# Attention with unnormalised probabilities, x's rows scaled by one over the sums, and a planner that knows a port and due work

## The chip, the cores and the metric

The kernel runs on one core of one Trainium2 chip. The metric is the device time of one execution in microseconds, as the median of the runs shown. The core's engines work side by side, each through its own queue in order: PE (TensorE, matrix products; PEld is its loading of weights), DVE (VectorE), ACT (ScalarE), POOL (GpSimd) and SP (SyncE), which issues the DMAs here.

## The reference, cut to what matters

```python
scores = q @ k.T / sqrt(64)                           # 4 batches, 8 heads, 576 rows, 64 wide
scores = causal(scores + cum[:, None] - cum[None, :]) # cum: running sum of log(clip(f))
attn = exp(scores - max(scores))
attn = attn / (sum(attn) + 1e-9)
x = concat_heads(attn @ v)                            # 2304 x 512
h = x @ w_in                                          # MoE1: 512 -> 1024
solu = h * softmax(h)
x = layernorm(solu) * g_ln @ w_out                    # 1024 -> 512
h = relu(x @ w2_in)                                   # MoE2: 512 -> 2048
out = (h * h) @ w2_out                                # 2048 -> 512
```

## The kernel before

**Precision.** The products of MoE1, MoE2 and the scores take each operand as a high part and a residual ("hi", "lo"), with three products for one in the MoEs. So every weight goes through `convert` once: a DMA of the raw words, an absolute value on ACT (L604), a scaling of the low words on whichever engine the planner picks (L283, L285 or L289), a shift (L608) and a merge (L612) on DVE, an add on POOL (L618), a high part cast on any engine (L281, L285 or L287) and a residual on POOL or DVE (L622).

**Work.** The 2304 tokens are cut into 20 attention tiles of 128 or 64 query rows (five for each batch). For each tile and each of 8 heads, `head` makes the scores in a bank Z (L465), finds the row's extreme value (L482, L485 on DVE), takes the exponential on ACT with the row sums beside it (L499), adds 1e-9 and inverts on DVE (L512 or L516, then L522), and multiplies the probabilities by that on POOL (L526). PE transposes them (L542), the result is copied to a PT buffer (L281, mostly on ACT), and `mix` multiplies by V, two heads at a time, into the bank XO (L563), which collects x, transposed. After the eighth head, XO is cast into XH (L281) and the residual XL is taken (L576). `first` then does MoE1's first product (L747 to L749, bank HP) and its softmax and layer norm; `out1` does the second product (L688 to L690) and stores x for MoE2. `step` does one of MoE2's 16 slices of the hidden width for a block of 384 tokens: 12 products up (L1019 to L1021), ReLU and square on ACT (L1027, L1029), a cast (L1030) and a residual (L1033) on DVE, 9 products down (L1049 to L1051).

**Stages.** MoE1's 24 weight pieces are converted beside the first attention tiles (`weights1`); MoE2's 64 pieces are converted after the last tile, into buffers that attention and MoE1 leave free (`weights2`), beside the first two blocks' steps. The other four blocks follow.

**The order of the work** comes from a planner, `Plan.lay`, when the kernel is built. Each group of instructions is a step with the engines that may do it, a cost on each, the steps it depends on and a priority (a due time: small goes first). `lay` simulates the engines; on each, of all steps that could start within 20 ns of the earliest, it takes the one with the smallest priority. The result is a fixed order for each engine. Semaphores keep the dependences; nothing keeps the simulated times.

```python
t0 = min(c[0] for c in cand)
c = min((c for c in cand if c[0] <= t0 + slack), key=lambda c: (c[1].prio, c[1].no))
```

A head's priority is its slot time. A piece of MoE2's weight slice fc is due at TEND - 3000 + 5000 fc, a step of block 0 at TEND - 2000 + 12000 fc, and one of block 1 15000 later.

Of the kernel before, what the change touches and what calls it, by code (L numbers as in the profile page):

```python
# [8 lines left out]
F32 = mybir.dt.float32  # L9
# [14 lines left out]
class Step:  # L24
    __slots__ = ("eng", "fn", "prio", "deps", "succ", "left", "rdy", "start", "end", "take", "uses", "on", "no", "late", "weak")


class Plan:
# [28 lines left out]
    def add(self, eng, fn, prio, reads=(), writes=(), take=None, uses=(), late=0):  # L57
# [8 lines left out]
        s.weak = None  # L66
# [29 lines left out]
    def lay(self, slack=60):  # L96
# [49 lines left out]
        todo = len(self.steps)  # L146
        order = []
        while todo:
            pick = None
            for e in engs:  # L150
                cand = []
                for s in avail[e]:
                    t = max(free[e], s.rdy[e])
                    if e == "dve" and len(s.eng) > 1:

                        o = min(max(free[x], s.rdy[x]) + s.eng[x] for x in s.eng if x != e)
                        if t + s.eng[e] + SHIFT > o:
                            continue
# [10 lines left out]
                c = min((c for c in cand if c[0] <= t0 + slack), key=lambda c: (c[1].prio, c[1].no))  # L169
                done = pe_end(c[0], c[1].eng[e], False) if e == "pe" else c[0] + c[1].eng[e]  # L170
# [7 lines left out]
            free[e] = done  # L178
            for a in s.eng:
                avail[a].remove(s)  # L180
# [14 lines left out]
def tile_kernel(ctx: ExitStack, tc: tile.TileContext, q, k, v, f, w_in, w_out, g_ln, w2_in, w2_out, out):  # L195
# [24 lines left out]
    NADJ, NPT, NV, NST = 3, 4, 6, 8  # L220
# [32 lines left out]
    ST = [new(f"st{i}", [8]) for i in range(NST)]  # L253
# [21 lines left out]
    def copy(n, dst, src, prio, reads, writes, uses=(), scale=None, psum=True):  # L275
# [20 lines left out]
        s = pl.add(ns, fn, prio, reads, writes, uses=uses)  # L296
# [28 lines left out]
    def att_ns(T):  # L325
        t, m = T["t"], T["m"]
        return 2 * max(107, T["ext"] / 2.4) + 53 + (t + 1) * m * (109 + 135) / 128 + 109

    EACH = 24 * 216 + 48 * 109 + 872
# [47 lines left out]
    def picks(i, j):  # L377
# [7 lines left out]
        s = pl.add(dict(dve=602, pool=1252), fn, -6.9e6 if i == 0 else 5000, ["ident"], [("qa", i, j)])  # L385

    def prep_k(n, prio):
# [5 lines left out]
        for j in range(2):  # L393
# [7 lines left out]
            def auxrows(y, j=j):  # L401
# [9 lines left out]
                dict(dve=67 + 1.045 * HH * m, pool=119 + 2.213 * HH * m), lo, prio + 2 * j, [("kn", j)] + hk, lk  # L411
# [8 lines left out]
    def prep_q(n, prio):  # L420
        m = tiles[n]["m"]
        i = n % 2
        for j in range(2):
# [14 lines left out]
            pl.add(dict(dve=67 + 1.045 * HH * m), lo, prio + 2 * j, [("qn", j), ("qh", i, j)], [("ql", i, j)])  # L438


    def head(s):
# [56 lines left out]
        def exp(y, c):  # L498
            nc.scalar.activation(  # L499
                out=adj[0:m, c[1] : c[2]], in_=Z[c[0]][0:m, 0 : c[2] - c[1]], func=AF.Exp, bias=st[0:m, low : low + 1],  # L500
                scale=-1.0, accum_out=st[0:m, 2 + y : 3 + y],
            )

        for y, (c, k_) in enumerate(zip(cuts, zk)):
            pl.add(
                dict(act=91 + 0.833 * (c[2] - c[1]) + 146), lambda y=y, c=c: exp(y, c), prio, [k_, sk_ + (low,)],
                [("adj", s % NADJ, y), sk_ + (2 + y,)], late=-110,
            )

        def total():  # L510
            if wide:
                nc.vector.scalar_tensor_tensor(  # L512
                    out=st[0:m, 4:5], in0=st[0:m, 2:3], scalar=1e-9, in1=st[0:m, 3:4], op0=ALU.add, op1=ALU.add
                )
            else:
                nc.vector.tensor_scalar_add(st[0:m, 4:5], st[0:m, 2:3], 1e-9)  # L516

        pl.add(
            dict(dve=69), total, prio - 300, [sk_ + (2 + y,) for y in range(len(cuts))], [sk_ + (4,)], late=93
        )  # L520
        pl.add(
            dict(dve=75), lambda: nc.vector.reciprocal(st[0:m, 5:6], st[0:m, 4:5]), prio - 300, [sk_ + (4,)], [sk_ + (5,)]  # L522
        )

        def norm():
            nc.gpsimd.tensor_scalar(  # L526
                out=adj[0:m, 0:ext], in0=adj[0:m, 0:ext], scalar1=st[0:m, 5:6], scalar2=1.0,
                op0=ALU.mult, op1=ALU.mult,
            )

        pl.add(dict(pool=244 + 0.833 * ext), norm, prio - 300, [sk_ + (5,)], ak)
# [20 lines left out]
    def mix(s):  # L552
# [17 lines left out]
        pl.add(dict(pe=(t + 1) * 270 * m / P), fn, prio, rk, ["xo"])  # L570
        if p == NP - 1:
            i = T["x"] % XB
            w = slice(off, off + m)

            def lo():
                nc.vector.tensor_tensor(  # L576
                    out=XL[i][:, :, w], in0=XO[:, :, w], in1=XH[i][:, :, w].bitcast(F32), op=ALU.subtract
                )

            copy(NP * m, lambda: XH[i][:, :, w], lambda: XO[:, :, w], prio, ["xo"], [("xh", i, off)])  # L580
            pl.add(dict(dve=67 + 1.045 * NP * m), lo, prio, ["xo", ("xh", i, off)], [("xl", i, off)])


    def convert(src, raw, w, hi, lo, n, prio, rawk, wk, outk, gain=None):
# [42 lines left out]
        pl.add(dict(dve=ts), a3, prio, [], [wk])  # L627
        pl.add(dict(dve=stt), a4, prio, [hk], [wk])
# [4 lines left out]
        m7 = pl.add(dict(pool=tt + 27, dve=stt), a7, prio, [wk, outk + ("h",)], [outk + ("l",)])  # L633
# [41 lines left out]
    def out1(blk, ccs, prio, dp):  # L675
# [3 lines left out]
        for cc in ccs:  # L679
            w = slice(cc * P, cc * P + P)  # L680
            sk = key()
            for g in range(4):
# [11 lines left out]
                pl.add(dict(pe=654), fn, prio, rk, [sk], take=sk if g == 0 else None, uses=[sk] if g else [])  # L694
# [37 lines left out]
    def first(x):  # L732
# [10 lines left out]
        for c in range(2):  # L743
            w = slice(c * 512, c * 512 + 512)
            for cc in range(KC):
                def fn(c=c, cc=cc, w=w):
# [5 lines left out]
                    dict(pe=648), fn, a + d * FH * (c * KC + cc) / 8, xk + [("wi", cc, c, y) for y in "hl"], ["h"]  # L752
# [135 lines left out]
    NRAW = NPT + 2  # L888
    raws = [(f"pt{i}", [("pt", i, g) for g in range(5)]) for i in range(NPT)]
    raws += [(f"adj{i}", [("adj", i, y) for y in range(2)]) for i in range(2)]  # L890
    wsl = [("adj2", 0), ("adj2", 256), ("xw", 0)]

    def weights2(fc, prio):
        pieces = places[fc]
        W2[fc] = [p[0] for p in pieces]
        for g in range(4):
# [106 lines left out]
    def step(blk, fc, prio):  # L1003
# [10 lines left out]
        for cc0 in range(0, KC, 2):  # L1014
            def up(cc0=cc0):
# [9 lines left out]
                dict(pe=6 * 162.5), up, prio, rk, [ck], take=ck if cc0 == 0 else None, uses=[ck] if cc0 else []  # L1025
# [273 lines left out]
```

## Time and profile before

| what | value |
|---|---|
| median of 3 runs | 905.02 us (904.74 to 905.56) |
| the profiled execution | 904.06 us, of which its span is 902.3 us |
| mean granted TensorE clock, as a share of 2.4 GHz | 0.98 |
| PE busy | 93% of the span |
| PEld busy | 80% |
| DVE busy | 56% |
| ACT busy | 52% |
| POOL busy | 39% |

How to read it: a share is a mean over stages with different limits. The views by stretch say which engine is full in each, the lists of waits say what PE waited for, and the groups of instructions say what one of a kind takes. The mean of a row contains the time for which an instruction, already begun, is held up. Line numbers such as L526 are those of the kernel before, unless it is said otherwise.

### The profile page before, as it was taken

What the parts mean: (1) busy time and instruction counts of PE and PEld (TensorE: products, weight loads), DVE (VectorE), ACT (ScalarE), POOL (GpSimd) and SP (SyncE); (2) the same over time, 40 slices, a digit from 0 to 9 for tenths busy, and PEclk for the clock granted to TensorE, in tenths of its full rate; (3) what the DMA queues carried; (4) which work ended last, traced back from release to release, by engine and by line L of the source; (5) the groups of instructions that cost most, each with busy time, mean ns of one, the idle gap of its engine ahead of it and who ended that gap; (6) DMA issues with size and microseconds to landing.
All of it is one profiled execution on the core that took longest, in us unless ns stands there. A gap on an engine that the chain in (4) does not pass through costs nothing.

```text
span 902.3 us, 15613 instructions
## 1 busy us (share of the span) xinstructions
PE 842.9 (93%) x5280; PEld 724.7 (80%) x5280; DVE 504.7 (56%) x1442; ACT 472.9 (52%) x1234; POOL 352.2 (39%) x508
## 2 busy tenths in 40 slices
PE   3878999999999999999979788999999999999998
PEld 1546887888888888788868677899989999899997
DVE  8998787666855677655799889322222222222221
ACT  5777767666766566665767666223322322322322
POOL 7988766433533456522588888100000000000000
PEclk9978898999999999999999999999999999999999
DMA  7733245222511125010545743005102002000000
GB/s 227 226 97 113 89 128 165 62 60 71 165 48 37 60 79 165 25 42 25 173 140 174 235 129 106 1 1 167 44 1 71 36 1 70 36 1 1 36 1 35
DMA packets 55503, 75.29 MB, mean 83 GB/s; under 512 B 7456, under 2 KB 35104, under 8 KB 55424
## 3 DMA queue, kind: packets, MB, share of 16 engines
q1 hardware_dynamic: 55424, 74.30, 26.6%
q8 instruction: 41, 0.67, 0.3%
q14 instruction: 38, 0.31, 0.1%
HBM read 59.91 MB, written 14.30 MB: 82 GB/s over the span
## 4 chain that ended last, share of the span: by engine, by line
PE 70%; DVE 13%; POOL 5%; issue 5%; DMA 4%; ACT 4%; SPq 1%; POOLq 0%; ACTq 0%; DVEq 0%
PE pp L1019 6%; PE pp L1021 6%; PE pp L1020 6%; PE pp L542 5%; PE z L465 5%; PE xo L563 5%; PE hp L747 3%; PE hp L749 3%; PE hp L748 3%; PE pp L688 3%; PE pp L689 3%; PE pp L690 3%; PE hp L1049 2%; PE hp L1050 2%; PE hp L1051 2%
## 5 line engine op out<-in xcount | busy, mean ns | idle before, releaser
L1030 DVE CAST q<-q 128x384 fp32r<-128x384 f32 x96 | 39.5, 411 | 251.5 <-PE pp L1051 92.2
L1027 ACT ACTIVATE q<-pp 128x384 f32<-128x384 f32 x96 | 47.1, 490 | 236.1 <-PE pp L1021 232.4
L526 POOL TENSOR_SCALAR adj<-adj,st 128x128 f32<-128x128 f32 (+9 forms) x160 | 100.2, 631 | 137.1 <-DVE st L522 96.7
L499 ACT ACTIVATE adj<-z,st 64x288 f32<-64x288 f32 (+9 forms) x192 | 95.7, 501 | 55.6 <-DVE st L485 36.7
L465 PE MATMUL z<-k,q 128*128 128x256 f32 (+17 forms) x384 | 98.7, 355 | 23.7 <-ACT adj L499 13.0
L281 ACT COPY pt<-pp 128x256 f32<-128x256 f32 (+5 forms) x176 | 72.3, 428 | 47.8 <-PE pp L542 45.8
L465 PEld LDWEIGHTS z<-k,q 128*128 128x128 f32 (+3 forms) x384 | 60.8, 192 | 36.8 <-ACT adj L499 18.9
L542 PE MATMUL pp<-ident,adj 128*128 128x128 f32 (+1 forms) x480 | 81.0, 284 | 9.2 <-POOL adj L526 8.3
L688 PE MATMUL pp<-ln,woh 128*128 128x256 f32 x288 | 83.4, 290 | 0.5 <-DVE ln L827 0.5
L485 DVE CUSTOM_DVE_ANT_0 z<-z,maskb 128x128 f32<-128x128 f32 (+8 forms) x144 | 65.5, 461 | 30.3 <-PE z L465 29.3
L690 PE MATMUL pp<-ln,woh 128*128 128x256 f32 x288 | 81.2, 282 | 0.0
L689 PE MATMUL pp<-ln,wol 128*128 128x256 f32 x288 | 81.2, 282 | 0.0
L542 PEld LDWEIGHTS pp<-ident,adj 128*128 128x128 f32 (+1 forms) x480 | 54.8, 145 | 31.3 <-POOL adj L526 16.5
L563 PE MATMUL xo<-pt,vn 128*64 128x128 f32 (+1 forms) x960 | 68.4, 279 | 0.0
L563 PEld LDWEIGHTS xo<-pt,vn 128*64 128x64 f32 x960 | 49.7, 141 | 21.6 <-issue 17.0
L747 PE MATMUL hp<-wih,xl 128*128 128x512 f32 x144 | 63.7, 442 | 1.1 <-ACT hp L786 0.6
L748 PE MATMUL hp<-wil,xh 128*128 128x512 f32 x144 | 58.9, 409 | 0.6 <-DVE st L516 0.6
L749 PE MATMUL hp<-wih,xh 128*128 128x512 f32 x144 | 58.6, 407 | 0.0
L688 PEld LDWEIGHTS pp<-ln,woh 128*128 128x128 f32 x288 | 54.7, 190 | 2.4 <-DVE ln L827 0.9
L689 PEld LDWEIGHTS pp<-ln,wol 128*128 128x128 f32 x288 | 54.7, 190 | 0.6
L690 PEld LDWEIGHTS pp<-ln,woh 128*128 128x128 f32 x288 | 54.4, 189 | 0.0
L1029 ACT ACTIVATE q<-q 128x384 f32<-128x384 f32 x96 | 50.3, 524 | 2.5
(479 smaller groups left out, 2238.2 us busy)
## 6 DMA issues: line engine op xcount, KB each, us to landing
x2d<-xc SPq DMA_DIRECT2D x72, 128.0 KB
kn<-in_k_dram SPq DMA_DIRECT2D x32, 256.0 KB
qn<-in_q_dram SPq DMA_DIRECT2D x32, 256.0 KB
pt<-in_moe_w_in_dram SPq DMA_DIRECT2D x22, 256.0 KB
pt<-in_moe_w_out_dram SPq DMA_DIRECT2D x22, 256.0 KB
vn<-in_v_dram SPq DMA_DIRECT2D x20, 256.0 KB
ln<-x2d SPq DMA_DIRECT2D x24, 192.0 KB
out_dram<-pt SPq DMA_DIRECT2D x18, 256.0 KB
```

The source lines that it names most:

```text
L281: nc.scalar.copy(dst(), src())
L465: nc.tensor.matmul(dst, lhsT=ql[0:r, p, 0:m], rhs=rhs, start=(g == 0), stop=(g == 1))
L499: nc.scalar.activation(out=adj[0:m, c[1] : c[2]], in_=Z[c[0]][0:m, 0 : c[2] - c[1]], func=AF.Exp, bias=st[0:m, low : low + 1], scale=-1.0, ...
L526: nc.gpsimd.tensor_scalar(out=adj[0:m, 0:ext], in0=adj[0:m, 0:ext], scalar1=st[0:m, 5:6], scalar2=1.0, op0=ALU.mult, op1=ALU.mult,)
L542: nc.tensor.transpose(at(sk)[:, (c - g) * m : (c - g + 1) * m], adj[0:m, zc : zc + P], ident[0:m, 0:m])
L563: nc.tensor.matmul(XO[own[j], p, off : off + m], lhsT=VN[vslot[b, c]][:, (2 * p + j) * D : (2 * p + j + 1) * D], rhs=pts[j][:, c * m : (c ...
L688: nc.tensor.matmul(px, lhsT=woh[:, fc, w], rhs=lo, start=(fc == 0), stop=False)
L689: nc.tensor.matmul(px, lhsT=wol[:, fc, w], rhs=hi, start=False, stop=False)
L690: nc.tensor.matmul(px, lhsT=woh[:, fc, w], rhs=hi, start=False, stop=(fc == KF - 1))
L747: nc.tensor.matmul(HP[:, c], lhsT=XL[i][:, cc, :], rhs=wih[:, cc, w], start=(cc == 0), stop=False)
L748: nc.tensor.matmul(HP[:, c], lhsT=XH[i][:, cc, :], rhs=wil[:, cc, w], start=False, stop=False)
L749: nc.tensor.matmul(HP[:, c], lhsT=XH[i][:, cc, :], rhs=wih[:, cc, w], start=False, stop=(cc == KC - 1))
```

## The change

**Attention.** The steps of L512, L516, L522 and L526 go: the exponentials are transposed and multiplied by V as they are. The row sums of the 8 heads of a tile are collected in a buffer `su`. At the end of a tile, eight sums at once get 1e-9 added and are inverted on DVE; a copy on any engine spreads the inverses, each 64 times, into a new buffer X (128 x 512); four transposes on PE (`spread`) and a copy from PSUM bring X into x's layout; one DVE multiply (`scaled`) takes XO times X into X; XH and XL are made from X, which lies in SBUF, so that POOL may do either.

**Planner.** A step marked `port` (most DVE operations with operands in SBUF alone, but not MoE2's L1030 and L1033) may not begin on DVE while POOL works in the simulation, and no POOL step begins while such a step runs on DVE. On the engines other than PE, where a step that becomes ready during the picked step is due by more than 400 earlier, and waiting for it wastes less time than it would be held up, it goes first, with something shorter put into the gap if that fits. Costs of PE's steps are set anew (a 512-column product 231 instead of 216 ns).

**Buffers.** PT buffers go from 4 to 3, the small ST buffers from 8 to 4, and X takes the place of one PT buffer as a landing place for MoE2's raw weights (still 6 in all). The causal mask is due earlier.

```diff
@@ Plan.lay
                     t = max(free[e], s.rdy[e])
+                    if e == "pool":
+                        t = max(t, port)
+                    elif e == "dve" and s.port and s.eng[e]:
+                        t = max(t, free["pool"])
...
+                if e != "pe":
+                    end = c[0] + c[1].eng[e]
+                    due = [
+                        x for x in cand
+                        if x[1].prio < c[1].prio - DUE and x[0] < end and end - x[0] > (x[0] - c[0]) * WORTH
+                    ]
+                    if due:
+                        x = min(due, key=lambda x: (x[1].prio, x[1].no))
+                        fits = [y for y in cand if y[0] + y[1].eng[e] <= x[0]]
+                        c = min(fits, key=lambda y: (y[1].prio, y[1].no)) if fits else x
...
+            if e == "dve" and s.port and s.eng[e]:
+                port = done
@@ copy
-        s = pl.add(ns, fn, prio, reads, writes, uses=uses)
+        s = pl.add(ns, fn, prio, reads, writes, uses=uses, port=not psum)
@@ tile_kernel
-    NADJ, NPT, NV, NST = 3, 4, 6, 8
+    NADJ, NPT, NV, NST = 3, 3, 6, 4
+    SU = [new(f"su{i}", [3, H]) for i in range(2)]
+    X = new("x", [NP, P])
@@ head
-                scale=-1.0, accum_out=st[0:m, 2 + y : 3 + y],
+                scale=-1.0, accum_out=su[0:m, y, h : h + 1],
...
-        pl.add(
-            dict(dve=75), lambda: nc.vector.reciprocal(st[0:m, 5:6], st[0:m, 4:5]), prio - 300, [sk_ + (4,)], [sk_ + (5,)]
-        )
...
-        pl.add(dict(pool=244 + 0.833 * ext), norm, prio - 300, [sk_ + (5,)], ak)
@@ mix, after a tile's last two heads
+            pl.add(dict(dve=72), total, prio - 300, sums, [uk])
+            pl.add(dict(dve=78), lambda: nc.vector.reciprocal(su[0:m, 2], su[0:m, 2]), prio - 300, [], [uk])
+            copy(
+                DM, lambda: X[0:m].rearrange("p c (j d) -> p (c j) d", d=D),
+                lambda: su[0:m, 2].unsqueeze(2).broadcast_to([m, H, D]), prio - 300, [uk], ["x"], psum=False,
+            )
+            pl.add(dict(pe=NP * 109 * m / P), spread, prio - 300, ["x", "ident"], [sk], take=sk)
+            copy(
+                NP * m, lambda: X[:, :, 0:m], lambda: at(sk).rearrange("p (c x) -> p c x", x=P)[:, :, 0:m], prio - 300,
+                [sk], ["x"], [sk],
+            )
+            pl.add(dict(dve=67 + 1.045 * NP * m), scaled, prio - 300, ["xo"], ["x"])
-            copy(NP * m, lambda: XH[i][:, :, w], lambda: XO[:, :, w], prio, ["xo"], [("xh", i, off)])
-            pl.add(dict(dve=67 + 1.045 * NP * m), lo, prio, ["xo", ("xh", i, off)], [("xl", i, off)])
+            copy(NP * m, lambda: XH[i][:, :, w], lambda: X[:, :, 0:m], prio, ["x"], [("xh", i, off)], psum=False)
+            l = pl.add(
+                dict(dve=67 + 1.045 * NP * m, pool=119 + 2.213 * NP * m), lo, prio, ["x", ("xh", i, off)], [("xl", i, off)],
+                port=True,
+            )
@@ weights2
-    NRAW = NPT + 2
+    NRAW = NPT + 3
+    raws += [("x", ["x"])]
@@ mask
-    pl.add(dict(pool=1480), mask, -6e6, ["ident"], ["mask", "e"])
+    pl.add(dict(pool=1480), mask, -8.95e6, ["ident"], ["mask", "e"])
+DUE, WORTH = 400, 1.0
```

**What moves, first place:** POOL beside the second attention tile, while MoE1's first weight is converted (`ln` is the staging buffer, `wih` and `wil` the weight's parts, `adj` the probabilities). Before:

```order
41 L526 TENSOR_SCALAR adj_32_99<-adj_32_99,st_37_104 128x256
42 L526 TENSOR_SCALAR adj_30_97<-adj_30_97,st_38_105 128x256
43 L285 TENSOR_SCALAR ln_52_163<-ln_52_163 128x512
44 L618 TENSOR_TENSOR ln_53_236<-ln_53_236 128x512
45 L526 TENSOR_SCALAR adj_31_98<-adj_31_98,st_39_106 128x256
46 L285 TENSOR_SCALAR wih_71<-ln_53_236 128x512
47 L618 TENSOR_TENSOR ln_52_163<-ln_52_163 128x512
48 L526 TENSOR_SCALAR adj_32_99<-adj_32_99,st_40_107 128x256
```

and with the change, in its own line numbers (L657 is the add, L661 a weight's residual, L421 K's residual, L307 any scaling or cast on POOL; `xh` is x's high part):

```order
27 L661 TENSOR_TENSOR wil_72<-ln_50_168,wih_71 128x512
28 L307 TENSOR_SCALAR xh_45_112<-x_109 128x512
29 L657 TENSOR_TENSOR ln_51_234<-ln_51_234 128x512
30 L421 TENSOR_TENSOR k_11_78<-kn_21_88,k_9_76 64x4x128
31 L307 TENSOR_SCALAR ln_50_168<-ln_50_168 128x512
32 L307 TENSOR_SCALAR q_16_83<-qn_22_89 64x512
33 L307 TENSOR_SCALAR q_17_84<-qn_23_90 64x512
34 L307 TENSOR_SCALAR k_8_75<-kn_20_87 128x4x128
35 L307 TENSOR_SCALAR k_9_76<-kn_21_88 128x4x128
```

The normalising multiplies are gone from between the conversions; more residuals stand on POOL, and the high parts of the weights have left it for ACT.

**Second place:** DVE while MoE2's weights are converted (`adj`, `xw`, `pt` and `x` hold pieces under conversion; the 128x384 rows are a step's cast and residual, into `q`, then `qn` or `kn`). Before:

```order
1180 L1030 CAST q_57_5617<-q_57_5597 128x384
1181 L608 TENSOR_SCALAR adj_56_4808<-adj_56_4808 128x256
1182 L1033 TENSOR_TENSOR qn_57_5628<-q_57_5597,q_57_5617 128x384
1183 L612 SCALAR_TENSOR_TENSOR adj_56_4808<-pt_56_4788,adj_56_4808 128x256
1184 L289 TENSOR_SCALAR pt_56_4869<-pt_56_4869 128x256
1185 L608 TENSOR_SCALAR adj_56_4808<-adj_56_4808 128x256
1186 L612 SCALAR_TENSOR_TENSOR adj_56_4808<-pt_56_4793,adj_56_4808 128x256
1187 L1030 CAST q_57_5656<-q_57_5597 128x384
1188 L608 TENSOR_SCALAR xw_4892<-xw_4892 128x256
1189 L1033 TENSOR_TENSOR qn_57_5668<-q_57_5597,q_57_5656 128x384
```

and with the change (L647 is the shift, L651 the merge, L1070 the cast, L1073 the residual):

```order
871 L647 TENSOR_SCALAR adj_54_4476<-adj_54_4476 128x256
872 L651 SCALAR_TENSOR_TENSOR adj_54_4476<-adj_54_4517,adj_54_4476 128x256
873 L1070 CAST q_55_4702<-q_55_4689 128x384
874 L1073 TENSOR_TENSOR kn_55_4706<-q_55_4689,q_55_4702 128x384
875 L647 TENSOR_SCALAR adj_54_4476<-adj_54_4476 128x256
876 L651 SCALAR_TENSOR_TENSOR adj_54_4476<-adj_54_4450,adj_54_4476 128x256
877 L647 TENSOR_SCALAR xw_4591<-xw_4591 128x256
878 L651 SCALAR_TENSOR_TENSOR xw_4591<-x_4581,xw_4591 128x256
879 L1070 CAST q_55_5340<-q_55_5323 128x384
880 L1073 TENSOR_TENSOR qn_55_5343<-q_55_5323,q_55_5340 128x384
```

A step's cast and its residual, and a piece's shift and its merge, now stand next to each other; before, a shift of another piece stood between. In the whole order 17 casts stood ahead of the last merge, and 20 do now.

## Rows read from the trace of the kernel before

**Rows 1.** The page, part 1: busy us (share of span) x instructions.

```profile
span 902.3 us, 15613 instructions
...
PE 842.9 (93%) x5280; PEld 724.7 (80%) x5280; DVE 504.7 (56%) x1442; ACT 472.9 (52%) x1234; POOL 352.2 (39%) x508
```

**Rows 2.** Four stretches: busy us of PE, PEld, DVE, ACT, POOL; clock, DMA, GB/s.

```profile
0.00:119.00 119.00, 88.30 (x508) 64.94 (x509) 105.77 (x279) 86.06 (x220) 100.75 (x142) 0.90 0.50 150
119.00:440.00 321.00, 316.99 (x2528) 266.94 (x2529) 211.03 (x796) 210.45 (x612) 143.24 (x226) 0.99 0.26 80
440.00:568.00 128.00, 107.00 (x597) 93.74 (x591) 114.76 (x210) 86.89 (x229) 106.70 (x140) 0.99 0.52 160
568.00:902.30 334.30, 330.62 (x1656) 299.06 (x1656) 73.12 (x159) 89.53 (x175) 1.54 (x2) 1.00 0.10 34
```

**Rows 3.** Waits of PE, 0 to 119 us: total us, times, longest.

```profile
PE z L465 <- ACT adj L499: 11.3, 7, 3.4
PE pp L542 <- POOL adj L526: 7.2, 11, 1.7
```

**Rows 4.** Two stretches, L526 on POOL alone: busy us (xcount).

```profile
0.00:119.00 119.00, 28.28 (x36) 0.90 0.50 150
119.00:440.00 321.00, 71.96 (x125) 0.99 0.26 80
```

**Rows 5.** First stretch, DVE lines L522, L516, L512 alone, in this order.

```profile
0.00:119.00 119.00, 5.53 (x36) 0.90 0.50 150
...
0.00:119.00 119.00, 4.45 (x32) 0.90 0.50 150
...
0.00:119.00 119.00, 1.49 (x4) 0.90 0.50 150
```

**Rows 6.** Groups by shape, POOL, 0 to 119 us: busy us, mean ns.

```profile
L285 POOL TENSOR_SCALAR ln<-ln 128x512 uint32<-128x512 uint32 x6 | 5.2, 874 | 2.1 <-DMA ln<-in_moe_w_in_dram 1.7
...
L622 POOL TENSOR_TENSOR wol<-xc,woh 128x256 fp32r<-128x256 f32 x6 | 4.6, 761 | 0.8 <-ACT woh L281 0.5
...
L285 POOL TENSOR_SCALAR wih<-ln 128x512 fp32r<-128x512 f32 x4 | 2.9, 737 | 0.1
...
L622 POOL TENSOR_TENSOR wil<-ln,wih 128x512 fp32r<-128x512 f32 x2 | 2.5, 1266 | 0.1
...
L285 POOL TENSOR_SCALAR woh<-xc 128x256 fp32r<-128x256 f32 x4 | 1.6, 404 | 0.1
```

**Rows 7.** Groups by shape, ACT, 0 to 119 us: the same columns.

```profile
L604 ACT ACTIVATE ln<-ln 128x512 f32<-128x512 f32 x8 | 5.4, 671 | 1.3 <-DMA ln<-in_moe_w_in_dram 1.3
...
L281 ACT CAST xh<-xo 128x512 fp32r<-128x512 f32 x4 | 2.3, 579 | 0.8 <-PE xo L563 0.8
...
L281 ACT CAST woh<-ws 128x256 fp32r<-128x256 f32 x5 | 2.0, 401 | 0.1
```

**Rows 8.** Lines L612 and L608 on DVE: ns min/median/max, first and last start.

```profile
L612 DVE SCALAR_TENSOR_TENSOR adj<-pt,adj x33: 417/793/947, 440.1 to 566.8; 128x256 uint32<-128x256 uint32 x33
...
L608 DVE TENSOR_SCALAR adj<-adj x43: 278/350/884, 439.7 to 565.7; 128x256 uint32<-128x256 uint32 x43
```

**Rows 9.** The chain of waits, 170 to 180 us: start, us, what.

```profile
175.43 0.87 PE pp L824 x8
```

**Rows 10.** Waits of PE, 119 to 440 us.

```profile
PE pp L542 <- POOL adj L526: 1.2, 3, 0.7
```

**Rows 11.** Waits of PE, 440 to 568 us.

```profile
PE hp L1049 <- DVE qn L1033: 8.6, 7, 2.3
PE z L1049 <- DVE kn L1033: 7.3, 5, 2.5
```

**Rows 12.** Two stretches, L1033 on DVE alone: busy us (xcount).

```profile
440.00:568.00 128.00, 15.06 (x17) 0.99 0.52 160
568.00:902.30 334.30, 44.12 (x79) 1.00 0.10 34
```

**Rows 13.** A stretch of 25 us, all engines: columns as in group 2.

```profile
600.00:625.00 25.00, 25.00 (x127) 22.79 (x126) 5.51 (x12) 6.71 (x14) 0.00 (x0) 1.00 0.23 72
```

More of the change, by code (lines that the diff above doesn't have):

```diff
@@ L24 @@
 class Step:
-    __slots__ = ("eng", "fn", "prio", "deps", "succ", "left", "rdy", "start", "end", "take", "uses", "on", "no", "late", "weak")
+    __slots__ = ("eng", "fn", "prio", "deps", "succ", "left", "rdy", "start", "end", "take", "uses", "on", "no", "late", "weak", "port")
 class Plan:
@@ L55, in __init__, with add @@
         self.slot = {}
-    def add(self, eng, fn, prio, reads=(), writes=(), take=None, uses=(), late=0):
+    def add(self, eng, fn, prio, reads=(), writes=(), take=None, uses=(), late=0, port=False):
         s = Step()
@@ L146, in lay @@
         todo = len(self.steps)
+        port = 0.0
         order = []
@@ L573, in mix, with total @@
             w = slice(off, off + m)
+            su = SU[n % 2]
+            sk = key()
+            wide = T["ext"] > 512
+            sums = [("su", n % 2, y, h) for y in range(1 + wide) for h in range(H)]
+            def total():
+                if wide:
+                    nc.vector.scalar_tensor_tensor(
+                        out=su[0:m, 2], in0=su[0:m, 0], scalar=1e-9, in1=su[0:m, 1], op0=ALU.add, op1=ALU.add
+                    )
+                else:
+                    nc.vector.tensor_scalar_add(su[0:m, 2], su[0:m, 0], 1e-9)
@@ L575, in lo, with spread, scaled @@
+            def spread():
+                tp = at(sk).rearrange("p (c x) -> p c x", x=P)
+                for c in range(NP):
+                    nc.tensor.transpose(tp[:, c, 0:m], X[0:m, c], ident[0:m, 0:m])
+            def scaled():
+                nc.vector.tensor_tensor(out=X[:, :, 0:m], in0=XO[:, :, w], in1=X[:, :, 0:m], op=ALU.mult)
             def lo():
-                nc.vector.tensor_tensor(
-                    out=XL[i][:, :, w], in0=XO[:, :, w], in1=XH[i][:, :, w].bitcast(F32), op=ALU.subtract
-                )
@@ L1054, in step @@
             pl.add(
-                dict(pe=648), down, prio + DOWN, rk, [bank], take=bank if slot and fc == 0 else None,
+                dict(pe=693), down, prio + DOWN, rk, [bank], take=bank if slot and fc == 0 else None,
                 uses=[bank] if slot and fc else [],
```

56 lines of the change are left out of this document (24 added, 32 removed).

## The prediction, made before the changed kernel ran

> **What bounds the kernel now.** I read the page's busy shares first [rows 1]: PE at 93% looks like the only limit. The profiled execution took 904.06 us, 1.76 more than its span, and stands 0.96 below the median of 905.02. The stretches come next [rows 2], and there the share falls apart into four stages. In the first, until MoE1's last weight is converted, PE is busy 88.3 of 119 us, while DVE is busy 105.8 and POOL 100.8: they set the pace. From 119 to 440 us PE is busy 317.0 of 321: it is the limit, and everything else hides. From 440 to 568 us MoE2's weights are converted; PE idles 21 us of 128, DVE (114.8) and POOL (106.7) are full again. After 568 us PE is alone with its work (330.6 of 334.3) and nothing in the change touches it.
>
> The waits of PE name the causes. In the first stretch it waited 11.3 us for exponentials and 7.2 us for the normalised probabilities [rows 3]; in the second 1.2 us for the latter [rows 10]; in the third 15.9 us for the two operands of MoE2's down products, made on DVE [rows 11].
>
> So the change can gain only in stretches one and three, and PE work that it adds costs its full price in stretch two.
>
> **Stretch one, the work removed and moved.** The counts are from the two orders, up to the last residual of MoE1's weights; both have the same 36 rows of least values of the heads on DVE by then.
>
> POOL loses 36 normalising multiplies, 28.3 us [rows 4]. Of MoE1's weights it gives away 5 scalings of 0.874, 4 casts of 0.737 and 6 of 0.404 us, 9.7 in all, and takes 3 residuals of 1.266 and 4 of 0.761, 6.8 in all [rows 6]. Of x it takes one spread, one cast and one residual, which the trace does not show; the nearest rows of the size (0.737, 0.737, 1.266) make 2.7. Together 28.3 + 9.7 - 6.8 - 2.7 = 28.5 less of 100.8.
>
> DVE loses the sums and inverses of every head, 5.5 + 4.5 + 1.5 = 11.5 us [rows 5], and the residuals that POOL takes; per tile it gets one multiply of the shape of the subtraction from PSUM that goes, and two small operations. At least 11.5 less of 105.8, so at most 94.
>
> ACT is the one that gets more: 34 instructions by the order, mostly these. Six of MoE1's w_in pieces at 0.671, four casts (I take the same 0.671), fourteen small ones at 0.401, and for x six more copies of 0.579 than before [rows 7], less four that go to DVE (0.579 each): 4.0 + 2.7 + 5.6 + 3.5 - 2.3 = 13.5, so 86.1 becomes about 99.6.
>
> What is late next is therefore ACT. DVE worked 89% of this stretch. With the then fullest engine at 94%, the stretch takes 99.6 / 0.94 = 106: **13 us gained**. At the limit, ACT without a gap, 99.6 us: 19.4, call it 20. At the other end, ACT at 86% of the stretch, 116 us: 3. I take 13, since the fullest engine of stretches one and three stands at 89 and 90%, and a plan with one more competitor gone should do a little better than these.
>
> PE was granted 0.90 of full clock here [rows 2], so about a fifth of it ran at 1.2 instead of 2.4 GHz. PE is not the limit there; I count nothing for the clock.
>
> **Stretch two, the work added to PE.** Four transposes for each of 20 tiles, 16 of them in this stretch, 4 of those half as wide. Eight of such a shape took 0.87 us on the chain [rows 9], so four 0.44: 12 x 0.44 + 4 x 0.22 = 6.2 us, all on the path. Against it PE no longer waits for normalised probabilities, 1.2 us [rows 10], and the way from exponential to transpose, which held DVE and POOL steps, is short; I take another 0.5 for waits that show on the loading of weights only. **Lost: 4.5 us**. Bounds: 1 (the shorter way hides most of it) and 9 (the spread comes late once in each of 16 tiles by 0.2). The wait that the change adds stands in PE's queue at those transposes: behind them are the last heads' products. In the order they stand ahead of the tile's last product into XO, so that X can be ready when XO is; XO is then read once instead of twice. On DVE the multiply waits for that product, and the next tile's least values stand behind it, as they stood behind the subtraction before. Three instead of four PT buffers hold two heads and the next; PE's order alternates transposes and products, and I cost it at nothing, covered by PE's own queue; were the cover gone, a wait would be of the 0.7 kind [rows 10], a few in all.
>
> SP issues as many DMAs as before (412 by the order), in other places; the row of output buffers, three for four, is used once in a block of three tiles. Nothing for both.
>
> **Stretch three.** The work stays: 64 pieces. POOL takes the eight residuals that DVE had, and gives low-word scalings to ACT, about even. What changes is the order on DVE. A step's cast and residual stand together, and 20 casts instead of 17 stand ahead of the last merge. A step is 21 products; PE does 127 in 25 us when alone [rows 13], so a step is 4.1 us and three more steps are 12.4 us of PE work that can fall into this stretch, where PE idles 21. I take two thirds: **8 us gained**. Bounds: 15 gained (all three, and part of the other waits) and 8 lost (the added POOL residuals lengthen 64 conversions by an eighth of a microsecond each).
>
> One rule speaks against it. The shift and the merge of one shape took 0.278 to 0.884 and 0.417 to 0.947 us, the merge 0.793 at the median [rows 8]: DVE holds an instruction until POOL lets go. The residual L1033 took 15.06 / 17 = 0.89 us here and 44.12 / 79 = 0.56 later, with POOL quiet [rows 12]. The Trainium skill (SBUF — State Buffer, "Who interferes with whom") says that DVE and GpSimd share one port pair as an exclusive lock, held for the whole instruction, and that the order of issue decides who is blocked. The trace agrees: one shape, twice the time beside POOL. By that rule a plan without semaphores for the port only renames the wait, and the third term would be zero; that is the first rival.
>
> **The sum.** -13 + 4.5 - 8 = -16.5 us; 904.06 - 16.5 = 887.6, and the median stands about 1 above its profiled execution: **888 us**. With its own bounds, 877 to 899.
>
> **The rivals.**
> 1. The lock stays. The planner's separation holds in its simulation alone, DVE's instructions stay as long as in [rows 8], and PE waits for L1033's results as long as now. For it: nothing in the change synchronises the two, and L1030 and L1033 are not marked. Against: the order itself differs by three steps. 904.06 - 13 + 4.5 = 895.6.
> 2. ACT becomes the limit of stretch one at once, and takes MoE2's scalings too: 3 gained, 4.5 lost, nothing in three: 905.6. For it: 99.6 us of work; against: ACT was idle 33 of 119 us.
> 3. Everything opens: the full 20 in stretch one, 1 lost, 15 gained: 870. For it: PE waited 18.5 us in stretch one for exactly what gets shorter [rows 3].
> 4. Slower. The new rule lets what is due earlier go first, and MoE2's pieces are due earlier than the steps that use them (5000 a slice against 12000). If DVE and ACT thereby serve the conversions first, the operands of the down products come later, and PE's 21 us of idle time double: 904.06 - 13 + 4.5 + 21 = 916.6. It decides from the point where PE idles more than 21 + 8.5 = 29.5 us in that stretch. Against: the order shows casts earlier, not later.
>
> **How the numbers follow.** Forecast 47%, lock 17%, ACT 8%, everything 20%, slower 8%. The range, 868 to 905, takes in the forecast's own, the first rival and most of the third, and leaves out the fourth, about half of the second and a third of the third: some 19%. Within 0.2% is 903.2 to 906.8, about what a measurement of this kernel can tell from no change. Faster: 46 of the forecast's 47, 16 of 17, 1 of 8, 20: 83%. Same: 1 + 0 + 5: 6%. Slower: 8 + 2 and a rest of 1: 11%.
>
> **What the profile of the changed kernel would show.** Stretch one right: the last residual of MoE1's weights ends near 106 instead of 120 us, POOL's busy time to there is some 72 us, ACT's 97 to 100. Wrong: it ends after 115, with ACT full. Stretch two right: PE above 98% busy and no wait of PE for the new transposes above 3 us in all. Stretch three right: the merges at a median well under 0.79 us and PE idle near 13 us; wrong: the merges as long as before (first rival) or PE idle above 29 us (fourth). The whole forecast is wrong if PE's last stretch, after the last MoE2 weight, grows by as much as the others shrink: then PE's own work, not the waits, sets the end.

## The result, and the profile after

The changed kernel takes 895.28 us (median, 894.71 to 896.65) against 904.88 for the kernel before, a ratio of 0.990 with a 95% interval of 0.989 to 0.992. That lies in the range, 7 us above the forecast, and almost on the number of the first rival (895.6). Neither working holds as written.

The page of the changed kernel, part 1, answers to [rows 1]: POOL lost 58 us, DVE 45, ACT gained 24, and PE, with 80 transposes more, is busy 1.5 us less.

```profile
span 892.9 us, 15185 instructions
...
PE 841.4 (94%) x5360; PEld 728.5 (82%) x5360; DVE 459.4 (51%) x1139; ACT 496.5 (56%) x1286; POOL 294.1 (33%) x379
```

The four stretches, cut where MoE1's conversion now ends and where MoE2's begins and ends, with the columns of [rows 2]:

```profile
0.00:118.00 118.00, 86.10 (x521) 64.85 (x522) 88.31 (x202) 96.10 (x247) 77.69 (x102) 0.91 0.48 149
118.00:434.00 316.00, 315.12 (x2565) 267.50 (x2564) 189.09 (x583) 217.50 (x620) 102.77 (x134) 1.00 0.26 80
434.00:573.00 139.00, 123.95 (x692) 109.54 (x691) 110.58 (x205) 95.59 (x250) 109.76 (x139) 0.98 0.49 152
573.00:892.90 319.90, 316.20 (x1589) 286.65 (x1587) 71.42 (x153) 87.27 (x172) 3.89 (x5) 1.00 0.11 35
```

The first stretch is 118 us where it was 119, though no helper is full in it now: DVE fell to 88.3 and ACT stands at 96.1. MoE2's conversion takes longer than before (139 us for 128), but PE works more beside it: 20 steps' residuals are made by its end, where 17 were.

The changed kernel's waits of PE from 0 to 118 us answer to [rows 3]. POOL's normalised probabilities are gone; exponentials still cost 9.8 us, and copies of transposed probabilities have joined. (Left out: the wait for the first query operand, 9.1 us, nearly all of it in the first 10 us.)

```profile
PE pp L543 <- ACT adj L523: 7.8, 8, 1.9
PE xo L564 <- ACT pt L303: 3.1, 4, 1.4
PE pp L727 <- ACT pt L303: 2.3, 1, 2.3
PE z L488 <- ACT adj L523: 2.0, 1, 2.0
```

The same view from 434 to 573 us answers to [rows 11]. As it stands, the operands of the down products, made on DVE, cost 5.3 us instead of 15.9, and ACT costs 9.1:

```profile
PE z L1089 <- ACT xw L643: 4.1, 2, 3.6
PE z L1089 <- ACT adj L643: 4.0, 1, 4.0
PE z L1089 <- DVE kn L1073: 3.2, 3, 1.7
PE hp L1089 <- DVE qn L1073: 2.1, 4, 0.7
PE z L1089 <- ACT k L303: 1.0, 1, 1.0
```

But a down product reads nothing that L643, the first step of a weight's conversion, writes. The view names whichever awaited engine signalled last, and the timeline shows what the product needed: it starts 0.15 us after the step's own residual L1073 ends, in a wait put down to ACT as in one put down to DVE (start us, us, what):

```profile
468.68 0.98 DVE L1073 TENSOR_TENSOR kn<-q,q 128x384 fp32r<-128x384 f32 x1
469.81 0.47 PE L1089 MATMUL z<-k,kn 128*128 128x512 f32 x1 [1.71 <-DVE kn L1073]
...
477.07 1.07 DVE L1073 TENSOR_TENSOR kn<-q,q 128x384 fp32r<-128x384 f32 x1
478.29 0.71 PE L1089 MATMUL z<-k,kn 128*128 128x512 f32 x1 [4.04 <-ACT adj L643]
```

The other waits put down to ACT (products at 452.24, 459.37 and 487.86) end 0.14 or 0.15 us after a residual as well. So the operands cost 14.4 us instead of 15.9.

The merges of MoE2's conversion by shape (the merge is L651 now, columns as in [rows 8]): three groups keep a median of 0.64 to 0.85 us, about as long as before; one is at 0.43. All 64 together take 41.9 us from 425 to 600, where they took 47.5.

```profile
L651 DVE SCALAR_TENSOR_TENSOR adj<-pt,adj x22: 411/426/965, 433.9 to 570.5; 128x256 uint32<-128x256 uint32 x22
L651 DVE SCALAR_TENSOR_TENSOR adj<-adj,adj x21: 415/854/966, 437.9 to 572.8; 128x256 uint32<-128x256 uint32 x21
L651 DVE SCALAR_TENSOR_TENSOR xw<-pt,xw x11: 412/847/958, 443.4 to 571.2; 128x256 uint32<-128x256 uint32 x11
L651 DVE SCALAR_TENSOR_TENSOR xw<-x,xw x10: 411/640/965, 448.4 to 564.6; 128x256 uint32<-128x256 uint32 x10
```

**A ledger for all kernels.** PE bounds the kernel, so I count what PE loses: the time in which it is not busy, and its busy time times one minus the granted clock. Three windows, to 150, 425 and 600 us, do for it. Of the kernel before:

```profile
0.00:150.00 150.00, 118.11 (x742) 88.64 (x742) 130.00 (x379) 109.61 (x299) 120.14 (x172) 0.90 0.50 152
150.00:425.00 275.00, 272.17 (x2166) 230.62 (x2166) 179.18 (x671) 176.68 (x500) 119.15 (x189) 1.00 0.23 70
425.00:600.00 175.00, 154.00 (x881) 135.26 (x880) 130.28 (x253) 104.64 (x276) 112.94 (x148) 0.99 0.41 125
```

and of the changed kernel:

```profile
0.00:150.00 150.00, 117.22 (x788) 88.97 (x788) 108.83 (x273) 120.94 (x330) 96.76 (x127) 0.93 0.48 149
150.00:425.00 275.00, 275.00 (x2237) 236.23 (x2236) 163.65 (x494) 186.69 (x516) 83.28 (x109) 1.00 0.24 72
425.00:600.00 175.00, 159.95 (x890) 141.22 (x889) 123.52 (x234) 108.84 (x285) 114.06 (x144) 0.98 0.40 125
```

To 150 us the kernel before loses 31.9 + 118.11 x 0.10 = 43.7, the changed one 32.8 + 8.2 = 41.0; then 2.8 and 0; then 22.5 and 18.2. The sum falls from 69.0 to 59.2 us, about what the profiled time fell by (904.06 to 895.01). The clock is printed to 0.01, so a figure is good to 1 or 2 us. Of the 9.8 us, 7.9 are idle time, all of it after 150 us (before that it rose from 31.9 to 32.8), and 1.9 the clock's.

### The profile page after: what moved, and what is told of

It is laid out like the page before. It is cut to its first block, busy times and chain, and to the rows that moved or that the text cites. A ratio compares the mean times of both kernels' runs of the same rounds, so it can differ in the third digit from the quotient of the medians.

```text
span 892.9 us, 15185 instructions
## 1 busy us (share of the span) xinstructions
PE 841.4 (94%) x5360; PEld 728.5 (82%) x5360; DVE 459.4 (51%) x1139; ACT 496.5 (56%) x1286; POOL 294.1 (33%) x379
## 4 chain that ended last, share of the span: by engine, by line
PE 77%; DVE 9%; DMA 5%; ACT 5%; issue 3%; POOL 2%; SPq 0%; POOLq 0%; DVEq 0%; ACTq 0%
PE pp L1059 6%; PE pp L1061 6%; PE pp L1060 6%; PE z L488 6%; PE pp L543 6%; PE xo L564 6%; PE pp L727 3%; PE hp L786 3%; PE hp L787 3%; PE hp L788 3%; PE pp L728 3%; PE pp L729 3%; PE hp L1089 2%; PE hp L1090 2%; PE hp L1091 2%
## 5 line engine op out<-in xcount | busy, mean ns | idle before, releaser
L1067 ACT ACTIVATE q<-pp 128x384 f32<-128x384 f32 x96 | 47.1, 491 | 223.1 <-PE pp L1061 221.0
L1070 DVE CAST q<-q 128x384 fp32r<-128x384 f32 x96 | 42.1, 438 | 243.4 <-PE xo L1091 92.3
L488 PE MATMUL z<-k,q 128*128 128x256 f32 (+17 forms) x384 | 95.1, 347 | 12.7 <-DVE q L456 9.1
L303 ACT COPY pt<-pp 128x384 f32<-128x384 f32 (+5 forms) x170 | 67.9, 420 | 39.0 <-PE pp L543 37.3
L543 PE MATMUL pp<-ident,adj 128*128 128x128 f32 (+1 forms) x480 | 78.7, 280 | 8.7 <-ACT adj L523 8.4
L543 PEld LDWEIGHTS pp<-ident,adj 128*128 128x128 f32 (+1 forms) x480 | 52.8, 143 | 30.2 <-ACT adj L523 19.4
L488 PEld LDWEIGHTS z<-k,q 128*128 128x128 f32 (+3 forms) x384 | 58.4, 188 | 19.7 <-ACT q L305 7.9
L564 PE MATMUL xo<-pt,vn 128*64 128x128 f32 (+1 forms) x960 | 70.3, 278 | 3.8 <-ACT pt L303 3.1
L564 PEld LDWEIGHTS xo<-pt,vn 128*64 128x64 f32 x960 | 50.6, 140 | 23.6 <-issue 11.8
L786 PE MATMUL hp<-wih,xl 128*128 128x512 f32 x144 | 61.5, 427 | 2.2 <-ACT hp L825 1.8
L307 POOL TENSOR_SCALAR q<-qn 64x512 fp32r<-64x512 f32 (+1 forms) x43 | 28.0, 652 | 55.3 <-PE z L488 50.0
```

The lines of the kernel that those rows point to most:

```text
L303: nc.scalar.copy(dst(), src())
L488: nc.tensor.matmul(dst, lhsT=ql[0:r, p, 0:m], rhs=rhs, start=(g == 0), stop=(g == 1))
L543: nc.tensor.transpose(at(sk)[:, (c - g) * m : (c - g + 1) * m], adj[0:m, zc : zc + P], ident[0:m, 0:m])
L564: nc.tensor.matmul(XO[own[j], p, off : off + m], lhsT=VN[vslot[b, c]][:, (2 * p + j) * D : (2 * p + j + 1) * D], rhs=pts[j][:, c * m : (c ...
L786: nc.tensor.matmul(HP[:, c], lhsT=XL[i][:, cc, :], rhs=wih[:, cc, w], start=(cc == 0), stop=False)
```

## Experiments

"Attention" below is the unnormalised probabilities, "port" the rule that keeps DVE and POOL apart, "due" the rule that lets what is due soon go first. "Attention" takes with it the new buffers; the planner's new costs and the earlier mask are in every kernel but the one before. Ratios are to the kernel before on the same chip. What is lost is read from the one profiled execution; in e1, e7 and e10 that one was 2 to 4 us faster than the median (904.57, 899.80 and 900.91), so the table may show too little lost there.

| kernel | attention, port, due | time, us | ratio, 95% interval | lost to 150 | 150 to 425 | 425 to 600 |
|---|---|---|---|---|---|---|
| before | no, no, no | 904.88 | 1 | 43.7 | 2.8 | 22.5 |
| e3 | yes, no, no | 904.61 | 1.0015 (1.0006 to 1.0023) | 36.8 | 0.8 | 27.8 |
| e9 | the same, other order | 904.47 | 1.0009 (0.9999 to 1.0019) | 37.3 | 1.4 | 28.7 |
| e2 | yes, no, yes | 911.35 | 1.0086 (1.0073 to 1.0099) | 38.3 | 1.9 | 33.1 |
| e1 | yes, yes, no | 906.57 | 1.0041 (1.0023 to 1.0058) | 48.2 | 6.2 | 13.9 |
| e10 | the same, other order | 904.95 | 1.0018 (0.9997 to 1.0040) | 46.8 | 3.9 | 14.9 |
| e4 | no, yes, yes | 903.72 | 0.9999 (0.9990 to 1.0009) | 42.1 | 0.8 | 23.1 |
| e11 | the same, other order | 904.26 | 1.0008 (0.9989 to 1.0028) | 45.6 | 3.9 | 18.4 |
| changed | yes, yes, yes | 895.28 | 0.9902 (0.9888 to 0.9916) | 41.0 | 0 | 18.2 |
| e5 | the same, other order | 887.67 | 0.9807 (0.9786 to 0.9827) | 39.6 | 0.3 | 13.1 |
| e6 | the same, other order | 892.07 | 0.9870 (0.9848 to 0.9891) | 39.6 | 0.1 | 16.5 |
| e8 | all, third staging buffer | 894.95 | 0.9885 (0.9863 to 0.9907) | 41.7 | 0.3 | 18.5 |
| e12 | all, ACT barred from copies | 903.97 | 1.0012 (1.0002 to 1.0021) | 47.1 | 3.6 | 18.1 |
| e7 | all, X transposed twice | 902.52 | 0.9984 (0.9964 to 1.0003) | 38.4 | 0 | 18.0 |

**e1 to e4: the parts apart.** e1 takes the due rule out of the changed kernel, e2 the port rule, e3 both; e4 is the kernel before with both rules, the marks, the planner's new costs and the earlier mask, but with probabilities normalised as before.

```diff
-                if e != "pe":            (e1, e3)
+                if False:
-        s.weak, s.port = None, port      (e2, e3)
+        s.weak, s.port = None, False
```

> The changed kernel without the rule that lets what is due soon go first. My theory now: the change's gain of about 9.6 us is made of an attention part worth some 3 to 5 us and a planner part (both rules and the costs) worth 5 to 6 us, all of it after 400 us; the due rule has perhaps half of that, so about 898 (895 to 902). Rival A, the planner's order changes nothing: 895. Rival B, the due rule is the whole planner part: 901 or more.

> The changed kernel with no step marked for the port, so that the planner keeps DVE and POOL apart nowhere. My theory now: the separation is worth the other half of the planner part, about 898 (895 to 902); the longest and the median merge of MoE2's conversion stay as they are (about 0.85 us), since no semaphore separates the engines. Rival A, the order changes nothing: 895. Rival B, the separation works on the chip: merges longer without it than with it, and 901 or more.

> The changed kernel with both planner rules off: what is left is the unnormalised probabilities, the tiles that go with them and the planner's new costs. My theory now: 900 (897 to 903), that is 4 to 5 us faster than before. Rival A, the whole gain comes from the attention part: 895. Rival B, the whole gain comes from the rules: 905.

> The kernel before with the planner's part of the change alone (both rules, the marks, the new costs, the earlier mask); probabilities are normalised as before. My theory now: 899 (896 to 903), and PE idles less than before after 425 us. Rival A, the whole gain comes from the attention part: 905. Rival B, the rules do it alone: 895.

All four came out at 903.7 to 911.4: neither the attention part alone (e3) nor the two rules alone (e4) gain anything, and taking either rule away costs the whole gain and more. My additive theory fell. e1 and e2 lie where their rivals B had them; e3 fits its rival B and e4 its rival A, and each of these gives the whole gain to the other part: what is left is that the parts need one another. The ledger says where. The attention part alone (e3) loses 7 us less to 150 us, all of it at the lower clock (3.5 us for 11.8; the idle time is 33.3 for 31.9), but 5 more in MoE2's conversion. The rows of e3:

```profile
0.00:150.00 150.00, 116.74 (x805) 87.63 (x805) 128.06 (x297) 108.20 (x304) 109.15 (x146) 0.97 0.51 156
150.00:425.00 275.00, 274.23 (x2221) 235.38 (x2220) 166.77 (x493) 186.28 (x522) 68.29 (x93) 1.00 0.23 69
425.00:600.00 175.00, 154.94 (x840) 135.61 (x839) 124.75 (x246) 102.21 (x266) 107.78 (x140) 0.95 0.39 124
```

The port rule on top (e1) takes MoE2's conversion from 27.8 to 13.9 lost (7.7 of the gain at the lower clock), but loses 11 more to 150 us and 5 in the next window, nearly all at the lower clock. The rows of e1:

```profile
0.00:150.00 150.00, 114.36 (x730) 87.62 (x730) 107.89 (x249) 114.31 (x305) 95.95 (x124) 0.89 0.48 147
150.00:425.00 275.00, 274.31 (x2183) 233.45 (x2183) 159.19 (x479) 191.11 (x540) 79.52 (x103) 0.98 0.24 72
425.00:600.00 175.00, 161.09 (x952) 141.74 (x949) 120.85 (x251) 114.71 (x303) 116.01 (x149) 1.00 0.40 127
```

The due rule without the port rule (e2) gains nothing. Both together give most of the good half of each: 41.0 lost to 150 us, and 18.2 in the conversion.

What the port rule does on the chip is seen in POOL's copies (the helper's line L307): busy time (xcount), clock, DMA share, GB/s, to 150 us and from 425 to 575. Of e3, then of the changed kernel:

```profile
0.00:150.00 150.00, 47.03 (x69) 0.97 0.51 156
425.00:575.00 150.00, 11.03 (x21) 0.94 0.46 144
```

```profile
0.00:150.00 150.00, 24.20 (x39) 0.93 0.48 149
425.00:575.00 150.00, 4.42 (x10) 0.98 0.47 146
```

The planner, which now counts POOL as blocked where a DVE step holds the port, hands some 40 copies to ACT; e1, with the port rule alone on top of e3, has 36 and 11 on POOL. The 64 merges of MoE2 get little shorter by it: 44.3 us in e3 and 44.6 in e2 without it, 40.7 in e1 but 45.3 in e10 with it. From 10 to 150 us PE waits 14.4 us for exponentials in e1 (10.4 in the changed kernel) and once 3.3 for w_out's cast on ACT. The first waits of PE in e1:

```profile
PE pp L543 <- ACT adj L523: 13.8, 11, 3.0
PE pp L727 <- ACT woh L303: 3.3, 1, 3.3
```

Neither rule shortens the wait for exponentials by itself: e3, with neither, waits 14.3 us, and e2, with the due rule alone, 15.0. With both it is 10.4, and 10.8 to 13.1 in e5, e6 and e8 below. So ACT's fuller queue is not what makes e1 wait. e3's smaller loss to 150 us is at the clock, 3.5 us for 12.6.

**e5 and e6: the same rules, another order.** A planner that lays thousands of steps may hit a good order by luck. Two edits without meaning lay it anew.

```diff
-                    dict(pe=693), fn, a + d * FH * (c * KC + cc) / 8, ...
+                    dict(pe=695), fn, a + d * FH * (c * KC + cc) / 8, ...
-                dict(pe=693), down, prio + DOWN, ...
+                dict(pe=695), down, prio + DOWN, ...
```

```diff
-POUT0, POUT = 50000.0, 2000
+POUT0, POUT = 50100.0, 2000
```

> The changed kernel with the planner's cost of a group of down or up products of MoE1 at 695 instead of 693 ns: a change without meaning, after which nearly every engine's order is laid anew. Theory P (the gain is that of this one order; each rule alone gave nothing because each re-lays the order, and the clock and the idle time of PE fall as they may): between 894 and 909, and different from 895.3 by more than 2 us. Theory R (the two rules work together, and the gain is theirs): within 2 us of 895.3.

> The changed kernel with the due times of MoE1's w_out pieces 0.1 us later (50100 for 50000): again nothing that matters, again another order. Theory P: between 894 and 909, not the same as the other such kernel. Theory R: within 2 us of 895.3. Under P the differences stand in the idle time of PE plus the time that it loses at the lower clock, which together are 62 us in the changed kernel's profile.

(The cost of e5 is that of MoE1's up products and MoE2's down products; the text on record names it wrongly.) Theory R's 2 us did not hold: chance of the order moves the time by several us, and by theory P's criterion both differ from 895.3. But both came out faster, below the 894 that P allowed: **e5 at 887.67 beats both kernels**, by changing 693 to 695 in two places. Its rows:

```profile
0.00:150.00 150.00, 118.74 (x812) 91.06 (x813) 113.12 (x283) 122.78 (x334) 99.00 (x129) 0.93 0.49 149
150.00:425.00 275.00, 274.69 (x2228) 235.84 (x2227) 165.61 (x497) 186.04 (x516) 82.32 (x108) 1.00 0.25 73
425.00:600.00 175.00, 163.54 (x909) 144.69 (x908) 123.94 (x230) 109.20 (x282) 113.78 (x144) 0.99 0.40 124
```

The gain over the changed kernel stands mostly in the last row, 5 of some 7 us: PE idles 11.5 us there instead of 15.1, and loses 1.6 for 3.2 at the lower clock.

**e9, e10, e11: is the lack of gain chance too?** Each is one of the kernels above with 695 for 693.

> The kernel of e3 (attention part, both rules off) with the cost 695 for 693 of e5 (MoE1's up products and MoE2's down products), that is another order of the same work. Theory P, every order lies anywhere between 887 and 911: this one may come below 896. Theory R, the rules together take 8 us or more from whatever order: 900 or more. Under R most of the loss stands in 425 to 600 us, where PE's idle time and its time lost at the lower clock together are 28 us in e3, 32 in e2, and 13 to 18 in the four orders with both rules.

> The kernel of e1 (attention part, port rule on, due rule off) with the cost 695. In e1 the stretch from 425 to 600 us was as good as with both rules (13.9 us lost), and 8.9 us more than in the changed kernel went to the lower clock before 425 us. If that was chance of the order (theory P for the due rule): 889 to 898. If the due rule is needed (theory R): 902 or more, with a clock loss of 15 us or more again.

> The kernel of e4 (planner's part on the kernel before) with the cost 695. If the rules gain only together with the attention part: 900 or more, like e4 (903.7). If e4 was an unlucky order: 890 to 898.

All three repeat their partners: 904.5, 905.0 and 904.3. So theory R holds in its main point. Of seven kernels without one of the three parts none has a median below 903; the four with all parts and nothing barred lie at 887.7 to 895.3. Theory P keeps the spread within that group. e10's clock loss came out at 12.9 us, not 15, in its profile, which is of its fastest execution. (The 8.9 us in e10's text is 9.9 by the ledger.) e2 was not repeated in another order, and the kernel before was laid neither in another order nor with the new costs alone, so how lucky its own order is stays open.

**e7: the price of the new transposes.** They are made twice, in the same order on every engine.

```diff
-                for c in range(NP):
+                for c in 2 * list(range(NP)):
                     nc.tensor.transpose(tp[:, c, 0:m], X[0:m, c], ident[0:m, 0:m])
```

> The changed kernel with the four new transposes of every tile made twice, in the same order on every engine (the planner's cost is left). If they are on the path at their full price, as my sum had it (0.44 us for four), the 80 more cost 8 to 9 us: 904. If PE's waits hide them in stretches one and three, 16 of 20 tiles remain: 902. Rival, they are hidden by the way of X through DVE and ACT: within 2 us of 895.3.

0.9984 - 0.9902 = 0.0082, or 7.4 us for 80, good to about 2: nearly the full price, so the rival fell. The first two guesses, 904 and 902, lie too close together to be told apart, so it stays open whether PE's waits hide a few of them.

**e8: a third staging buffer for w_out.**

```diff
-            i = g % 2
+            i = g % 3 if g < 14 else g % 2
-                lambda stage=stage: stage()[:, 512:768], ...
+                (lambda: XCS()[:, 768:1024]) if i == 2 else (lambda stage=stage: stage()[:, 512:768]), ...
```

> The changed kernel with a third staging buffer for the first 14 of w_out's 16 pieces (raw words where the last rows of the low words will stand, the working words in the free quarter of the first buffer). Theory S (the chain of each piece through two buffers sets the end of the conversion, 4.0 us a piece): the last residual of MoE1's weights ends 10 us earlier or more, before 108 us instead of 118. Rival, ACT sets it (92% busy from 60 to 100 us): it ends after 114. For the time: the order is laid anew, so 894 to 909 under theory P; under theory R it gains what PE's idle time to 150 us falls by, 3 us or more.

The last residual of MoE1's weights, in the changed kernel (ns, first and last start):

```profile
L661 POOL TENSOR_TENSOR wol<-xc,woh x8: 726/740/1050, 64.6 to 113.2; 128x256 fp32r<-128x256 f32 x8
L661 POOL TENSOR_TENSOR wol<-ws,woh x8: 728/732/744, 67.2 to 117.2; 128x256 fp32r<-128x256 f32 x8
```

and in e8:

```profile
L669 POOL TENSOR_TENSOR wol<-xc,woh x10: 725/739/897, 64.7 to 107.7; 128x256 fp32r<-128x256 f32 x10
L669 POOL TENSOR_TENSOR wol<-ws,woh x6: 725/732/939, 66.1 to 111.0; 128x256 fp32r<-128x256 f32 x6
```

It starts at 111.0 instead of 117.2. Other orders with two buffers do not do that (116.8 in e5, 116.6 in e6), so it is the buffer. It falls between the two expectations, so the buffers are a part of what sets the end and not the whole. What counts is that PE gained nothing by it: 41.7 us lost to 150 us for 41.0, and the time is the same within the spread.

**e12: ACT barred from the casts and scalings of MoE1's weights.**

```diff
+        act = rawk[0] == "2r"
-        copy(n, hi, w, prio, [wk], [outk + ("h",)], (), None, False)
+        copy(n, hi, w, prio, [wk], [outk + ("h",)], (), None, False, act)
```

> The changed kernel with ACT barred from the casts and the two scalings of MoE1's weight conversion (DVE and POOL take all of them, one or two engines' choice of the planner). Theory A (ACT, busy 92% from 60 to 100 us, is what PE waits for in stretch one, 7.8 us for exponentials): PE's idle time to 150 us falls from 32.8 us to 27 or less. Rival L (what PE waits for is the way from scores to transposed probabilities itself, whoever is free): it stays within 2 us of 32.8, with ACT below 75% busy from 60 to 100 us. The time follows the order: 885 to 905 either way.

PE idles 34.4 us to 150 us, within the rival's 2 us, so theory A fell; but ACT is at 80% from 60 to 100 us, not below 75. PE waits longer for exponentials with a freer ACT: 12.5 + 4.5 us from 10 to 150 for 8.4 + 2.0. Its waits:

```profile
PE pp L545 <- ACT adj L525: 12.5, 13, 3.1
...
PE z L490 <- ACT adj L525: 4.5, 3, 2.1
```

ACT's load alone is not what makes these waits. The whole gain was lost with this edit, 6 us of it to 150 us and 3.6 in the next window, some 7 of these at the lower clock. That fits the port rule, which has the copies on ACT; but it is one order, and not shown to be the reason.

## Why the prediction was right, and where its steps failed

- **The loads of stretch one: right.** POOL 77.7 us (some 72 forecast, so 23 less and not 28.5), ACT 96.1 (97 to 100), DVE 88.3 (at most 94).
- **What I made of them: wrong.** The step that failed is "with the then fullest engine at 94%, the stretch takes 106 us: 13 gained". It ended at 118, my own sign of failure, but not with ACT full, 81%. I took the end of the conversion as set by an engine's load, and a shorter stretch as PE's gain. e8 shows both links broken: the end moves with the staging buffers, and PE does not follow. PE lost 2.7 us less to 150 us, not 13, and idled 0.9 us more. That the time still lies in the range is in good part luck.
- **"I count nothing for the clock": wrong in size.** The loss at the lower clock fell from 11.8 to 8.2 us to 150 us, more than the whole gain there, and rose from 1.5 to 3.2 after 425.
- **Stretch two, +4.5: right in size, with an open remainder.** Its signs came true: PE was 99.7% busy, and waited 1.9 us for the new transposes in the whole run. From 150 to 425 us the 52 transposes of the changed kernel were busy 7.6 us (line, shapes, count; busy us, mean ns with the shared pipeline; idle):

```profile
L591 PE MATMUL pp<-ident,x 128*128 128x128 f32 (+1 forms) x52 | 7.6, 269 | 0.0
```

The idle time fell by 2.8: +4.8. PE never waited for them there, and e7 confirms the price. Yet what is left of the span after the ledger hardly rose, from 833.2 to 833.7 us, where e7's is 841.3. So some 7 us of PE's busy time went elsewhere, or 4 to 5 when the clock is read in windows of 5 us, which round less (831.6 and 834.6). One mean points to the time before 150 us: there a first product of MoE1 (L747, now L786) took 499 ns and takes 439, but 428 and 425 from 150 to 425. Whether that is the clock alone stays open.
- **Stretch three, -8: half the size, and not by the wait that I named.** Three more steps did fall into the stretch, 20 for 17. But a residual there takes no less (19.71 us for 20 from 425 to 573, so 0.99; it was 0.89 [rows 12]), and the waits for the down products' operands, from which the gain was to come, fell only from 15.9 to 14.4 us. Most of the idle time that went is other waits of before, 3.1 us of it one wait for the load of x:

```profile
PE pp L1019 <- DMA ln<-x2d: 3.1, 1, 3.1
```

Measured: -4.3, with 1.7 more at the lower clock taken in. The sign "merges well under 0.79 us" failed for two of the four groups, and PE idles 15.1 us where 13 were forecast. So the first rival was right in its premise, merges and waits about as long as before, and wrong in its conclusion that nothing then moves: e1 and e10 against e3 and e9 show the port rule worth 14 us in this window, about half of it idle time and half at the lower clock. That it works through the engine that a copy goes to fits these runs, but no run fixed that alone. The Trainium skill (SBUF — State Buffer, "Who interferes with whom") has one port pair shared by DVE and GpSimd as an exclusive lock. The merges' 0.85 us with the rule on agree that a plan does not lift it.
- **The sum.** I added an attention part of -8.5 and a planner part of -8. Neither exists alone (e3 and e9, e4 and e11). The "own bounds" of 877 to 899 do not follow from the terms' bounds, which add to 870 and 918. That 895.28 lies on the first rival's 895.6 is chance: that was -13, +4.5 and 0, and the ledger reads -2.7, -2.8 and -4.3. The ACT rival (905.6) named the engine that carries the new load, but it was not the limit; the slower rival's mechanism, the due rule serving conversions first, would fit e2 alone, which has that rule without the port rule (33.1 us lost in the third window, 911.4); no run tests it.

## What to carry to other kernels

Where a planner lays the order, the terms of a change do not add: test the parts by taking one out, and lay each version in two or three orders by an edit without meaning before crediting a rule with a per cent. Here three orders of the same rules spread over 7.6 us, and one of them was the best kernel of the study. A stretch in which the helpers are full does not get shorter for the bounding engine because they get emptier: ask which wait of that engine ends last, and count its time at the lower clock beside its idle time. Before a wait is put down to the engine that a view names, check in the timeline that the instruction reads what that engine wrote.

## What the runs showed of the hardware

The clock's part was larger than I had thought. In e1 PE is idle for 3.86 of 5 us at 117.5, after which the clock is low, on and off, to 137; at 140 it idles 1.01 of 2.5, and from 142.5 the granted clock falls to 0.50, the lower level of 1.2 GHz, and stays there to 160 us although PE is busy throughout. All engines as in [rows 2]:

```profile
117.50:120.00 2.50, 0.76 (x7) 0.56 (x5) 1.89 (x3) 0.48 (x1) 1.55 (x3) 1.00 0.66 210
120.00:122.50 2.50, 0.38 (x1) 0.19 (x1) 1.76 (x2) 1.37 (x4) 2.30 (x4) 1.00 0.00 0
...
140.00:142.50 2.50, 1.49 (x25) 1.09 (x25) 2.01 (x11) 2.29 (x8) 1.98 (x4) 1.00 0.48 130
142.50:145.00 2.50, 2.50 (x27) 1.92 (x23) 1.54 (x6) 1.99 (x10) 1.97 (x3) 0.64 0.92 254
145.00:150.00 5.00, 5.00 (x23) 3.21 (x21) 2.09 (x8) 2.73 (x10) 1.15 (x2) 0.50 0.82 266
150.00:155.00 5.00, 5.00 (x20) 4.05 (x21) 3.13 (x10) 2.81 (x11) 2.46 (x3) 0.50 0.20 51
155.00:160.00 5.00, 5.00 (x28) 4.54 (x26) 0.68 (x3) 1.70 (x6) 0.40 (x1) 0.50 0.26 91
160.00:165.00 5.00, 5.00 (x44) 4.12 (x44) 3.66 (x12) 3.71 (x14) 1.35 (x2) 0.97 0.24 64
```

Of the 17.5 us from 142.5 on 8.4 are lost; just before stands a gap of one. Over the kernels here the loss at the lower clock to 150 us runs from 3.5 us (e3) to 12.7 (e12) at nearly the same idle time (33.3 and 34.4): where the gaps come counts, not only their sum.
